# Keys and queries of a gated linear-attention kernel projected in three column blocks of 384 in place of four of 288

## The chip, the core and the metric

The kernel runs on one core of a Trainium2 chip. The core has engines with queues of their own: TensorE (PE for its matmuls, PEld for the weight loads that run beside them), VectorE (DVE), ScalarE (ACT), GpSimd (POOL) and SyncE (SP), which here only issues transfers. The metric is the device time of one execution in microseconds.

## What is computed

With x of 2048 rows and 576 columns, the reference mixes two branches by a gate for each row:

```python
def _A_ref(x, wqkv, wo):                      # linear attention, 32 heads of 18 columns
    qkv = (x @ wqkv).reshape(B, S, 3, H, Dh).transpose(2, 0, 3, 1, 4)
    q, k, v = qkv[0], qkv[1], qkv[2]
    phi = lambda t: jnp.where(t > 0, t + 1, jnp.exp(t)) + 1e-6
    pq, pk = phi(q), phi(k)
    kv = jnp.einsum("bhsd,bhse->bhde", pk, v)
    z = jnp.einsum("bhsd->bhd", pk)
    num = jnp.einsum("bhqd,bhde->bhqe", pq, kv)
    den = jnp.einsum("bhqd,bhd->bhq", pq, z)[..., None] + 1e-6
    return (num / den).transpose(0, 2, 1, 3).reshape(B, S, D) @ wo

def _B_ref(x, w1, b1, w2, b2):                # MLP, 576 -> 4608 -> 576
    h = _gelu(jnp.einsum("bsd,df->bsf", _layernorm(x), w1) + b1)
    return jnp.einsum("bsf,fd->bsd", h, w2) + b2

g = _sigmoid((x * gate_w).sum(-1, keepdims=True))
return g * _A_ref(x, wqkv, wo) + (1 - g) * _B_ref(x, w1, b1, w2, b2)
```

## The kernel before

The rows of x are cut into 16 tiles of 128. Every matmul works on numbers split into a high and a low part, so that one product is a sum of several. The 576 rows of the contraction are four slices of 128 and one of 64; with the parts this gives 14 matmuls for one block of output columns. `HI_FIRST = HH + LH + TAIL + HL` and `BY_ROWS` are two orders of the same 14: HH and TAIL need the high parts of weights and x, LH the low part of x, HL the low part of the weights, and the second matmul of TAIL a low part of the last weight slice.

**The first stage** goes over the tiles once. For each tile it projects keys and queries, applies phi, and adds to the sums that linear attention needs. Keys (576 columns) and queries (576) are each projected in two halves of 288 columns (`HALF`), so that a tile takes four blocks of 14 matmuls, 56 in all. The second half of the keys is two columns wider: the gate's weights and a column of ones stand there, and `sums_of_x` reads the gate's sum and the row's mean out of them. `phi` reads a block from its bank of ps: two ACT activations (relu of the negative, then exp) into e, and one DVE operation that puts max(p, 0) + e into k or into the tile's acc. `keys_split` and `split_xn` make high and low parts (ks, xs), and `add_products` adds the tile's 19 products into six banks of ps, in two parts of 8 and 11 matmuls. Blocks of projections alternate between banks 6 and 7 (`halves_in`). In the loop over tiles FIRST to 15, the order on PE is: keys of tile n, first part of the products of tile n-1, queries of tile n, second part of these products. Work for the MLP's input (`Y_JOBS`) is hung in by hand at 48 numbered places, three to a tile. The queries of the last `LATE` = 3 tiles are left for later: one after the loop, one after the sums have been copied out, one behind the transposes of the first normalized tile.

**The start** is written out by hand for the first three tiles. SP issues the loads of x (`load_x`, into t, one transfer for four slices and two for the last) and of the weights (`load_w`, into s); the first block of key weights is issued by ACT itself, in pieces, ahead of its table load and its first copies. `split_w` and `split_x` make the high part by ACT and the low part by DVE. Before that, PE multiplies a tile of ones 12 times (`WARM`). First all keys of the first block go to PE, then those of the second.

The framework counts transfers on eight counters, DMAHW0 to DMAHW7. A transfer that takes a counter in use waits on the issuing engine until the one before it on that counter has landed; whatever stands behind it on that engine waits too.

**Later stages**: the sums are finished and projected by wo, each tile's queries are normalized, transposed and multiplied (`attend`), and then the MLP runs for some 830 us, its instructions put in order by a planner that works on fixed costs in the code. The change does not touch that planner.

Of the kernel before, what the change touches and what calls it, by code (L numbers as in the profile page):

```python
# [9 lines left out]
F32 = mybir.dt.float32  # L10
F32R = mybir.dt.float32r
AF = mybir.ActivationFunctionType
OP = mybir.AluOpType
# [4 lines left out]
P = 128  # L18
S, D, H, DH, F = 2048, 576, 32, 18, 4608
NT = S // P  # L20
HALF = D // 2
# [14 lines left out]
EPS_LN = 1e-5  # L36
WARM = 12
FIRST = 3
LATE = 3
X_RING = 4  # L40
LAST_SHARE = 7

# [5 lines left out]
HI_FIRST = HH + LH + TAIL + HL  # L48
BY_ROWS = [p for pair in zip(HH, HL) for p in pair] + TAIL + LH
# [56 lines left out]
def half_cols(half):  # L106
    return slice(half * HALF, (half + 1) * HALF)
# [19 lines left out]
def tile_gated_mix(ctx: ExitStack, tc: tile.TileContext, x, xm, xe, wm, we, wvm, wve, wo, um, ue, w2, b1, b2, gw, out):  # L127
    nc = tc.nc
    pe, act, dve, pool = (InOrder(tc, e) for e in (nc.tensor, nc.scalar, nc.vector, nc.gpsimd))
    sp = InOrder(tc, nc.sync)  # L130
# [5 lines left out]
    ps = ctx.enter_context(tc.tile_pool(name="ps", bufs=1, space=PSUM)).tile([P, 8, 512], F32, name="ps")  # L136
# [60 lines left out]
    QUERY, KEY = range(2)  # L197
    W, at_ = {}, 0
    for part in (KEY, QUERY):
        for half in range(2):  # L200
            n = HALF + 2 * (part == KEY and half)
            W[part, half] = ym[:, at_:at_ + 10 * n].rearrange("p (a n) -> p a n", n=n)
            at_ += 10 * n
# [12 lines left out]
    yt = a1b.enter_context(tc.tile_pool(name="yt", bufs=3))  # L216
    xnp = a1b.enter_context(tc.tile_pool(name="xnp", bufs=2))
    kp = a1b.enter_context(tc.tile_pool(name="kp", bufs=2))
    wsp = wsc.enter_context(tc.tile_pool(name="wsp", bufs=4, side="right"))
    wraw, xs, xraw, xnraw = {}, {}, {}, {}  # L220

    def load_w(part, half, pieces=((0, 5),), by=sp):
        if (part, half) not in wraw:
            wraw[part, half] = wsp.tile([P, 5, HALF + 2], F32, name="s", tag="s")
        s = wraw[part, half]
        main = wm[part * 2 + half].rearrange("p (t n) -> p t n", t=4)
        tail = we[part * 2 + half]
# [6 lines left out]
    def split_w(part, half, by=dve, pieces=((0, 5),)):  # L234
        w = W[part, half]
        s = wraw[part, half][:, :, :w.shape[2]]
# [28 lines left out]

    halves_in, banks = cycle((6, 7)), {}

    def project(i, part, half, order=BY_ROWS, n=None, between={}):
        w = W[part, half]
        p = banks[i, part, half] = ps[:, next(halves_in) if n is None else n]  # L270
# [5 lines left out]
    def projected(i, part):  # L276
        for half in range(2):
            project(i, part, half)
# [12 lines left out]
    def keys_phi(i, half):  # L291
        if half == 0:
            K[i] = kp.tile([P, D], F32, name="k")
        phi(K[i], i, KEY, half, (lambda: None, lambda: sums_of_x(i))[half])

    def sums_of_x(i):
        own = slice(PLACE[i], PLACE[i] + 1)
        act.activation(gsum[:, own], banks[i, KEY, 1][:, HALF:HALF + 1], AF.Copy)
        act.activation(nmean[:, own], banks[i, KEY, 1][:, HALF + 1:HALF + 2], AF.Copy, scale=-1 / D)

    def sum_keys(i):
        if i != ORDER[0]:
# [16 lines left out]
            dve.tensor_sub(to[:, at_:at_ + c1 - c0], xnraw[i][:, c0:c1], raw(to[:, c0:c1]))  # L319

    def queries_out(i):
        for half in range(2):
            phi(acc[i], i, QUERY, half)


    KC = 448
# [136 lines left out]
    load_xn(first[0])  # L463
    load_w(QUERY, 1)
    load_xn(first[1])
    pool.memset(mask, 1.0)
    blocks = heads(mask)
# [5 lines left out]
    split_w(KEY, 0, pieces=((0, 1), (1, 2)))  # L473
    split_x(first[0], ((4, 5),))
    split_w(KEY, 0, pieces=((2, 4), (4, 5)))

    def first_keys(n, half, between={}):
        project(first[n], KEY, half, HI_FIRST, 3 * half + n, between)

    def first_queries(n, half):  # L480
        project(first[n], QUERY, half, HI_FIRST)

    def both_phi(n):
        for half in range(2):
            keys_phi(first[n], half)


    column = ps[:, 7, :5]
# [13 lines left out]
    dve.tensor_copy(wraw[KEY, 1][:, :, HALF:HALF + 1], column[:, :, None])  # L502
    dve.memset(wraw[KEY, 1][:, :, HALF + 1:HALF + 2], 1.0)
    split_w(KEY, 1)
    split_x(first[2])
    load_x(ORDER[3])
    first_keys(0, 1)
    first_keys(1, 1)
    both_phi(0)
    split_w(QUERY, 0)  # L510
    first_keys(2, 0)
    first_keys(2, 1)
    both_phi(1)
    keys_split(first[0])
    first_queries(0, 0)
    first_queries(1, 0)
    both_phi(2)
    phi(acc[first[0]], first[0], QUERY, 0)
    split_xn(first[0])
    moments_of(first[0])  # L520
    load_xn(first[2])
    first_queries(2, 0)
    phi(acc[first[1]], first[1], QUERY, 0)
    for part in range(2):
        add_products(first[0], part)
    split_w(QUERY, 1)
    phi(acc[first[2]], first[2], QUERY, 0)
    first_queries(0, 1)
    first_queries(1, 1)
    keys_split(first[1])  # L530
    split_xn(first[1])
    moments_of(first[1])
    load_xn(ORDER[FIRST])
    phi(acc[first[0]], first[0], QUERY, 1)
    add_products(first[1], 0)
    phi(acc[first[1]], first[1], QUERY, 1)
    first_queries(2, 1)
    split_x(ORDER[3])
    load_x(ORDER[4])
    load_x(ORDER[5])  # L540
    add_products(first[1], 1)
    phi(acc[first[2]], first[2], QUERY, 1)
    keys_split(first[2])
    split_xn(first[2])
    wsc.close()
# [51 lines left out]
    for n in range(FIRST, NT):  # L597
        i, before = ORDER[n], ORDER[n - 1]
        if n + 3 < NT:
            load_x(ORDER[n + 3])  # L600
        project(i, KEY, 0)
        keys_phi(i, 0)
        project(i, KEY, 1)
        if n + 1 < NT:
            split_x(ORDER[n + 1])
        keys_phi(i, 1)
        moments_of(before)
        if n + 1 < NT:
            load_xn(ORDER[n + 1])
        keys_split(i)  # L610
        add_products(before, 0)
        split_xn(i)
        run(3 * n)
        if n < NT - LATE:
            projected(i, QUERY)
# [7 lines left out]
    projected(late[0], QUERY)  # L623
    queries_out(late[0])
    moments_of(end)
    for part in range(2):
# [125 lines left out]
    normalize(2, (0,))  # L752
    transpose_q(0)
    normalize(2, (1,))
    for half in range(2):
# [861 lines left out]
```

## Time and profile before

| | |
|---|---|
| timed runs | 1095.13, 1095.46 and 1095.92 us, median 1095.46 |
| profiled execution | span 1094.1 us from its first to its last instruction; its own time around the span is not listed apart |
| PE | busy 1087.8 us of the span, 6694 matmuls |
| DVE, ACT, POOL | 917.2, 687.5, 235.6 us |
| mean granted clock | 0.999 |
| projections of keys and queries | 896 matmuls: 672 of 288 columns and 224 of 290 |

The page gives busy time by engine, the chain of work that ended last, and groups of instructions. The timeline lists instructions in order of time, those of one kind merged: start, length, engine (with q: its queue, which issues transfers), operation, tile written and tile read, shape, how many, and in brackets the idle time before and what ended it. Nearly all instructions have the line of one helper, L120, so the tiles tell them apart. A matmul's length overlaps the next one's; the pace is read from start to start.

### The profile page before, as it was taken

The numbers are of one execution on the slowest core, as the hardware profiler recorded it, in microseconds if no ns is written. First come the engines' busy times: TensorE is split into PE (matmuls) and PEld (weight loads), VectorE is DVE, ScalarE is ACT, GpSimd is POOL, SyncE is SP. The second block draws the span as 40 slices with busy tenths as digits, with TensorE's granted clock in tenths as the row PEclk, the third lists the DMA queues.
The fourth block names the chain that finished last, engine by engine and source line by source line (L and its number), as shares of the span: only waits on it lengthen the run. The fifth ranks groups of instructions, "written<-read, shape, count | busy, mean of one in ns | idle before, by whom it ended". The sixth has DMA issues, their size and how long they took to land.

```text
span 1094.1 us, 18599 instructions
## 1 busy us (share of the span) xinstructions
PE 1087.8 (99%) x6694; PEld 996.8 (91%) x6694; DVE 917.2 (84%) x1553; ACT 687.5 (63%) x1230; POOL 235.6 (22%) x232
## 2 busy tenths in 40 slices
PE   9999999999999999999999999999999999999998
PEld 9999999999898889988889999989899999999898
DVE  4568784895799999899999997988887888878888
ACT  6677765454667887777877876455545555455552
POOL 2111112531123232332111202121122211221110
PEclk9999999999999999999999999999999999999999
DMA  6466772745745565764556559574444435444432
GB/s 186 128 88 190 171 218 102 286 173 188 252 152 195 184 206 192 235 215 161 199 174 222 195 192 395 174 253 119 138 145 118 130 119 150 132 119 119 135 100 87
DMA packets 109006, 189.72 MB, mean 173 GB/s; under 512 B 8940, under 2 KB 68604, under 8 KB 104818
## 3 DMA queue, kind: packets, MB, share of 16 engines
q1 hardware_dynamic: 108002, 187.78, 53.3%
q8 instruction: 53, 0.87, 0.3%
q10 hardware_dynamic: 720, 0.74, 0.2%
q14 instruction: 39, 0.32, 0.1%
q0 software_dynamic: 192, 0.01, 0.1%
HBM read 121.70 MB, written 66.80 MB: 172 GB/s over the span
## 4 chain that ended last, share of the span: by engine, by line
PE 93%; DVE 3%; DMA 1%; ACT 1%; issue 0%; SPq 0%; ACTq 0%; DVEq 0%
PE ps L120 93%; DVE accs L120 1%; DMA s<-in_wm 0%; DVE h L120 0%; DMA fresh<-in_ue 0%; DMA ystage<-late_acc 0%; ACT u L120 0%; DMA s<-in_we 0%; DVE wp L120 0%; DVE region L120 0%; SPq L120 0%; DVE den L120 0%; DVE fresh L120 0%; DVE ystage L120 0%; DVE u L120 0%
## 5 line engine op out<-in xcount | busy, mean ns | idle before, releaser
L120 PEld LDWEIGHTS ps<-region,h 128*128 128x128 f32 x3072 | 437.8, 188 | 30.1 <-ACT ps L120 4.3
L120 PE MATMUL ps<-region,h 128*128 128x288 f32 x3072 | 457.1, 296 | 1.0 <-DVE region L120 0.4
L120 DVE TENSOR_TENSOR accs<-ps,accs 128x576 f32<-128x576 f32 x330 | 246.1, 753 | 60.9 <-PE ps L120 54.1
L120 PE MATMUL ps<-y,wa 128*128 128x512 f32 x1008 | 257.6, 393 | 0.0
L120 PEld LDWEIGHTS ps<-y,wa 128*128 128x128 f32 x1008 | 180.9, 188 | 30.3 <-ACT ps L120 0.2
L120 POOL TENSOR_TENSOR fresh<-fresh 128x288 f32<-128x288 f32 (+1 forms) x128 | 116.4, 913 | 410.5 <-DMA fresh<-in_w 129.6
L120 PE MATMUL ps<-y,wb 128*128 128x512 f32 x756 | 199.3, 394 | 0.1
L120 DVE TENSOR_TENSOR h<-u,h 128x512 fp32r<-128x512 f32 x240 | 165.9, 704 | 8.7 <-ACT u L120 8.7
L120 PEld LDWEIGHTS ps<-y,wb 128*128 128x128 f32 x756 | 133.9, 188 | 20.9 <-ACT u L120 0.5
L120 ACT ACTIVATE region<-fresh 128x576 fp32r<-128x576 f32 (+1 forms) x132 | 81.3, 625 | 73.5 <-PE ps L120 72.9
L120 PE MATMUL ps<-y 128*128 128x288 f32 (+1 forms) x896 | 125.8, 297 | 0.3 <-DVE y L120 0.2
L120 PEld LDWEIGHTS ps<-y 128*128 128x128 f32 x896 | 122.6, 189 | 1.8 <-DVE y L120 0.4
L120 ACT ACTIVATE ps<-ps 128x576 f32<-128x576 f32 (+1 forms) x127 | 78.7, 621 | 45.0 <-PE ps L120 21.5
L120 POOL TENSOR_TENSOR u<-u 128x512 f32<-128x512 f32 x44 | 57.0, 1296 | 193.5 <-DVE h L120 54.9
L120 DVE TENSOR_TENSOR region<-fresh,region 128x576 fp32r<-128x576 f32 (+1 forms) x132 | 93.8, 723 | 1.1 <-ACT region L120 1.1
L120 ACT ACTIVATE u<-ps 128x512 f32<-128x512 f32 x73 | 43.0, 589 | 68.4 <-PE ps L120 68.2
L120 ACT ACTIVATE h<-u 128x512 fp32r<-128x512 f32 x128 | 73.5, 622 | 10.0 <-DVE u L120 5.5
L120 ACT ACTIVATE h<-u,b1s 128x512 fp32r<-128x512 f32 x73 | 52.6, 722 | 42.6 <-DVE u L120 42.4
L120 PE MATMUL ps<-wp,qt 128*128 128x288 f32 x448 | 63.0, 297 | 0.0
L120 DVE TENSOR_TENSOR u<-ps,u 128x512 f32<-128x512 f32 x74 | 50.4, 683 | 13.5 <-PE ps L120 12.7
L120 PEld LDWEIGHTS ps<-wp,qt 128*128 128x128 f32 x448 | 59.8, 188 | 0.0
L120 DVE TENSOR_TENSOR u<-u 128x512 f32<-128x512 f32 x84 | 58.1, 691 | 1.7 <-POOL u L120 1.1
(137 smaller groups left out, 1052.1 us busy)
## 6 DMA issues: line engine op xcount, KB each, us to landing
w1d<-wa SPq DMA_DIRECT2D x17, 1280.0 KB
wa<-w1d SPq DMA_DIRECT2D x68, 320.0 KB
fresh<-in_w SPq DMA_DIRECT2D x70, 288.0 KB
y<-yd SPq DMA_DIRECT2D x14, 1280.0 KB
w1d<-wb SPq DMA_DIRECT2D x17, 960.0 KB
wb<-w1d SPq DMA_DIRECT2D x51, 320.0 KB
yd<-ystage SPq DMA_DIRECT2D x28, 320.0 KB
fresh<-in_um SPq DMA_DIRECT2D x64, 128.0 KB
```

Source lines behind the costliest of these rows:

```text
L120: self.last = self.tc.keep_in_program_order(op(*args, **kwargs))
```

## The change

Keys and queries of a tile are taken as one row of 1152 columns and cut into three blocks of 384 (`BLOCK`): block 0 is keys 0 to 383, block 1 the other 192 keys and the first 192 queries (`REST` = 192) with the two extra columns (386 wide), block 2 the other 384 queries. The first 192 query columns of each tile, late tiles too, are so projected with its keys. The weights still lie in memory as four pieces of 288 columns (Q0, Q1, K0, K1), so each block is loaded from two of them. `LATE` becomes 4: the fourth late block goes with the last one into banks 4 and 5. At the start, all blocks 2 of the first three tiles are projected one after another, and the products of the first and second tile follow without a projection between.

```diff
-LATE = 3
+LATE = 4
+BLOCK = 384
+REST = D - BLOCK
...
-    wsp = wsc.enter_context(tc.tile_pool(name="wsp", bufs=4, side="right"))
+    wsp = wsc.enter_context(tc.tile_pool(name="wsp", bufs=3, side="right"))
...
+    Q0, Q1, K0, K1 = range(4)
+    EDGE = BLOCK - HALF
+    SOURCES = (((K0, 0, HALF), (K1, 0, EDGE)), ((K1, EDGE, HALF), (Q0, 0, REST)), ((Q0, REST, HALF), (Q1, 0, HALF)))
+
+    def load_w(n, pieces=((0, 5),), by=sp):
+        if n not in wraw:
+            wraw[n] = wsp.tile([P, 5, BLOCK + 2], F32, name="s", tag="s")
         for t0, t1 in pieces:
-            if t0 < 4:
-                by.dma_start(s[:, t0:min(t1, 4), :HALF], main[:, t0:min(t1, 4)])
-            if t1 == 5:
-                load_twice(s[:, 4, :HALF], tail, by)
+            to = 0
+            for i, c0, c1 in SOURCES[n]:
+                s = wraw[n][:, :, to:to + c1 - c0]
+                to += c1 - c0
+                if t0 < 4:
+                    by.dma_start(s[:, t0:min(t1, 4)], wm[i].rearrange("p (t n) -> p t n", t=4)[:, t0:min(t1, 4), c0:c1])
+                if t1 == 5:
+                    load_twice(s[:, 4], we[i][:, c0:c1], by)
...
-    def phi(dst, i, part, half, also=lambda: None):
+    def phi(i, n, outs, also=lambda: None):
-        p, own = banks[i, part, half][:, :HALF], half_cols(half)
-        e = tmp.tile([P, HALF], F32, name="e")
-        act.activation(e, p, AF.Relu, scale=-1.0)
+        p = banks[i, n]
+        e = tmp.tile([P, BLOCK], F32, name="e")
+        act.activation(e, p[:, :BLOCK], AF.Relu, scale=-1.0)
         act.activation(e, e, AF.Exp, scale=-1.0)
         also()
-        dve.scalar_tensor_tensor(dst[:, own], p, 0.0, e, op0=OP.max, op1=OP.add)
+        c0 = 0
+        for dst in outs:
+            c1 = c0 + dst.shape[1]
+            dve.scalar_tensor_tensor(dst, p[:, c0:c1], 0.0, e[:, c0:c1], op0=OP.max, op1=OP.add)
+            c0 = c1
...
-    def keys_phi(i, half):
-        if half == 0:
+    def keys_phi(i, n):
+        if n == 0:
             K[i] = kp.tile([P, D], F32, name="k")
-        phi(K[i], i, KEY, half, (lambda: None, lambda: sums_of_x(i))[half])
+            phi(i, 0, [K[i][:, :BLOCK]])
+        else:
+            phi(i, 1, [K[i][:, BLOCK:], acc[i][:, :REST]], lambda: sums_of_x(i))
...
     def queries_out(i):
-        for half in range(2):
-            phi(acc[i], i, QUERY, half)
+        phi(i, 2, [acc[i][:, REST:]])
...
-    load_w(KEY, 0, ((0, 1), (1, 2), (2, 4)), act)
+    load_w(0, ((0, 1), (1, 2), (2, 4)), act)
...
-    load_w(KEY, 0, ((4, 5),), act)
+    load_w(0, ((4, 5),), act)
     load_x(first[1])
-    load_w(KEY, 1)
+    load_w(1)
     load_x(first[2])
-    load_w(QUERY, 0)
+    load_w(2)
...
-    project(late[1], QUERY, 0, n=4)
-    project(late[1], QUERY, 1, n=0)
+    project(late[1], 2, at_=4)
...
-    for half in range(2):
-        project(late[2], QUERY, half, n=4 + half)
+    for n in range(2):
+        project(late[2 + n], 2, at_=4 + n)
     transpose_q(1)
     tail_q(2)
     queries_out(late[2])
+    queries_out(late[3])
```

The first place is ACT's queue at the very start. Rows name the tile written and the tensor read, the shape of one instruction, and in brackets what it waits for; in_wm and in_we hold the four main slices and the last slice of the weights. Before, ACT has three pieces and the last slice, twice, to issue:

```order
L120 DMA s<-in_wm 128x288 x2
L120 DMA s<-in_wm 128x2x288
L120 ACT_TABLE_LOAD
L120 ACTIVATE tiny<-ones 128x1 [waits DVE_49]
L120 DMA s<-in_we 64x288 [waits DMAHW1_49]
L120 DMA s<-in_we 64x288 [waits DMAHW3_49]
L120 ACTIVATE y<-t 128x512
```

After the change, on the same engine, from its third instruction on (the first two are the pieces of 288 and 96 columns of the slice before):

```order
L122 DMA s<-in_wm 128x288
L122 DMA s<-in_wm 128x96
L122 DMA s<-in_wm 128x2x288 [waits DMAHW0_49]
L122 DMA s<-in_wm 128x2x96 [waits DMAHW2_49]
L122 ACT_TABLE_LOAD
L122 ACTIVATE tiny<-ones 128x1 [waits DVE_49]
L122 DMA s<-in_we 64x288 [waits DMAHW6_49]
L122 DMA s<-in_we 64x288 [waits DMAHW0_49]
L122 DMA s<-in_we 64x96 [waits DMAHW2_49]
L122 DMA s<-in_we 64x96 [waits DMAHW3_49]
L122 ACTIVATE y<-t 128x512 [waits DMAHW1_49]
```

ACT issues ten transfers where it issued five, and six of them wait for a counter where two did, all ahead of its table load or of its first copy.

The second place is SP's queue behind the loads of x for the first two tiles, up to the load of x for the third; here the second block of weights is issued. Before:

```order
L120 DMA t<-in_xe 64x128 [waits DMAHW0_49]
L120 DMA s<-in_wm 128x4x288 [waits DMAHW2_49]
L120 DMA s<-in_we 64x288 [waits DMAHW4_49]
L120 DMA s<-in_we 64x288 [waits DMAHW5_49]
L120 DMA t<-in_xm 128x512 [waits DMAHW6_49]
```

After:

```order
L122 DMA t<-in_xe 64x128 [waits DMAHW3_49]
L122 DMA s<-in_wm 128x4x192 [waits DMAHW4_49]
L122 DMA s<-in_we 64x192 [waits DMAHW5_49]
L122 DMA s<-in_we 64x192 [waits DMAHW7_49]
L122 DMA s<-in_wm 128x4x192 [waits DMAHW1_49]
L122 DMA s<-in_we 64x192 [waits DMAHW4_49]
L122 DMA s<-in_we 64x192 [waits DMAHW5_49]
L122 DMA t<-in_xm 128x512 [waits DMAHW6_49]
```

Three transfers became six, and the load of x for the third tile stands behind all of them.

More of the change, by code (lines that the diff above doesn't have):

```diff
@@ L196, in tile_gated_mix @@
     Y = ym.rearrange("p (m j s n) -> p m j s n", m=7, j=TPB, s=5)
-    QUERY, KEY = range(2)
-    W, at_ = {}, 0
-    for part in (KEY, QUERY):
-        for half in range(2):
-            n = HALF + 2 * (part == KEY and half)
-            W[part, half] = ym[:, at_:at_ + 10 * n].rearrange("p (a n) -> p a n", n=n)
-            at_ += 10 * n
+    W, at_ = [], 0
+    for n in (BLOCK, BLOCK + 2, BLOCK):
+        W.append(ym[:, at_:at_ + 10 * n].rearrange("p (a n) -> p a n", n=n))
+        at_ += 10 * n
     y_place = ym[:, at_ + X_RING * 9 * P:][:, :2 * 5 * P]
@@ L218, in tile_gated_mix, with split_w @@
     kp = a1b.enter_context(tc.tile_pool(name="kp", bufs=2))
-    wsp = wsc.enter_context(tc.tile_pool(name="wsp", bufs=4, side="right"))
+    wsp = wsc.enter_context(tc.tile_pool(name="wsp", bufs=3, side="right"))
     wraw, xs, xraw, xnraw = {}, {}, {}, {}
[L222 to L227, printed above, removed]
-        for t0, t1 in pieces:
-            if t0 < 4:
-                by.dma_start(s[:, t0:min(t1, 4), :HALF], main[:, t0:min(t1, 4)])
-            if t1 == 5:
-                load_twice(s[:, 4, :HALF], tail, by)
-    def split_w(part, half, by=dve, pieces=((0, 5),)):
-        w = W[part, half]
-        s = wraw[part, half][:, :, :w.shape[2]]
+    Q0, Q1, K0, K1 = range(4)
[4 more added lines that the diff above has]
+            wraw[n] = wsp.tile([P, 5, BLOCK + 2], F32, name="s", tag="s")
+        for t0, t1 in pieces:
+            to = 0
[6 more added lines that the diff above has]
+                    load_twice(s[:, 4], we[i][:, c0:c1], by)
+    def split_w(n, by=dve, pieces=((0, 5),)):
+        w = W[n]
+        s = wraw[n][:, :, :w.shape[2]]
         for t0, t1 in pieces:
@@ L266, in tile_gated_mix, with project @@
     halves_in, banks = cycle((6, 7)), {}
-    def project(i, part, half, order=BY_ROWS, n=None, between={}):
-        w = W[part, half]
-        p = banks[i, part, half] = ps[:, next(halves_in) if n is None else n]
+    def project(i, n, order=BY_ROWS, at_=None, between={}):
+        w = W[n]
+        p = banks[i, n] = ps[:, next(halves_in) if at_ is None else at_]
         for m, (a, b) in enumerate(order):
@@ L472, in tile_gated_mix, with first_keys, first_queries @@
     split_x(first[0], ((0, 4),))
-    split_w(KEY, 0, pieces=((0, 1), (1, 2)))
+    split_w(0, pieces=((0, 1), (1, 2)))
     split_x(first[0], ((4, 5),))
[L475 to L481, printed above, removed]
+    split_w(0, pieces=((2, 4), (4, 5)))
+    def first_keys(n, block, between={}):
+        project(first[n], block, HI_FIRST, 3 * block + n, between)
+    def first_queries(n):
+        project(first[n], 2, HI_FIRST)
     def both_phi(n):
-        for half in range(2):
-            keys_phi(first[n], half)
+        for block in range(2):
+            keys_phi(first[n], block)
     column = ps[:, 7, :5]
@@ L501, in tile_gated_mix @@
     first_keys(1, 0)
[L502 to L504 removed]
+    dve.tensor_copy(wraw[1][:, :, BLOCK:BLOCK + 1], column[:, :, None])
+    dve.memset(wraw[1][:, :, BLOCK + 1:BLOCK + 2], 1.0)
+    split_w(1)
     split_x(first[2])
@@ L514, in tile_gated_mix @@
     keys_split(first[0])
-    first_queries(0, 0)
-    first_queries(1, 0)
+    first_queries(0)
+    first_queries(1)
     both_phi(2)
-    phi(acc[first[0]], first[0], QUERY, 0)
+    queries_out(first[0])
     split_xn(first[0])
@@ L521, in tile_gated_mix @@
     load_xn(first[2])
-    first_queries(2, 0)
-    phi(acc[first[1]], first[1], QUERY, 0)
+    first_queries(2)
+    queries_out(first[1])
     for part in range(2):
         add_products(first[0], part)
[L526 to L529, printed above, removed]
     keys_split(first[1])
@@ L533, in tile_gated_mix @@
     load_xn(ORDER[FIRST])
-    phi(acc[first[0]], first[0], QUERY, 1)
+    queries_out(first[2])
     add_products(first[1], 0)
-    phi(acc[first[1]], first[1], QUERY, 1)
-    first_queries(2, 1)
     split_x(ORDER[3])
@@ L622, in tile_gated_mix @@
     late, end = ORDER[NT - LATE:], ORDER[-1]
-    projected(late[0], QUERY)
+    project(late[0], 2)
     queries_out(late[0])
```

18 lines of the change are left out of this document (6 added, 12 removed).

## The prediction

> **What bounds the kernel now.** I read the page first, then the stages by windows, then PE's waits, then the chain of waits, and last the timeline of the first 14 us and of one tile of the loop.
>
> ```profile
> PE 1087.8 (99%) x6694; PEld 996.8 (91%) x6694; DVE 917.2 (84%) x1553; ACT 687.5 (63%) x1230; POOL 235.6 (22%) x232
> ```
>
> ```profile
> 55.00:166.00 111.00, 111.00 (x739) 106.47 (x738) 84.95 (x182) 80.18 (x180) 18.08 (x14) 1.00 0.68 166
> 166.00:201.00 35.00, 34.84 (x220) 31.23 (x219) 18.61 (x44) 14.61 (x33) 8.01 (x6) 1.00 0.37 130
> 201.00:1094.00 893.00, 888.28 (x5390) 807.71 (x5388) 785.48 (x1263) 555.59 (x937) 199.25 (x192) 1.00 0.53 177
> ```
>
> The columns are stretch, length, then PE, PEld, DVE, ACT and POOL. In the loop over tiles PE is busy for all of 111.00 us, while DVE stands at 84.95 and ACT at 80.18. In the stretch behind it PE loses 0.16 us. So in the stage that the change touches PE is the bound: what makes its work shorter is gained, what makes it start later is lost, and work taken from ACT and DVE is worth nothing.
>
> ```profile
> 1.74 5.12 DMA s<-in_wm
> 6.88 0.48 SPq L120
> 7.40 2.97 DMA s<-in_we
> 10.47 1.43 ACT y L120
> 11.93 1.68 DVE y L120
> 13.65 179.71 PE ps L120 x1201
> ```
>
> The chain (start, length, what) shows where a late start would come in: transfers of weights, ACT's copy and DVE's rest of them, and from 13.65 us on PE alone for 180 us. Nothing gives back a delay before 13.65.
>
> **The change part by part: the matmuls.** The columns that PE must stream stay the same, since 4 x 288 = 3 x 384. What falls away is a fixed share of each matmul: 42 for 56 in each of 16 tiles.
>
> ```profile
> 59.70 1.58 PE L120 MATMUL ps<-ks,xs 128*128 128x448 f32 x7
> 61.12 3.90 PE L120 MATMUL ps<-y 128*128 128x288 f32 x28
> 64.86 0.85 PE L120 MATMUL ps<-xs,ks 128*128 128x512 f32 x3
> 65.54 1.23 PE L120 MATMUL ps<-ks,xs 128*128 128x512 f32 x5
> 66.61 3.88 PE L120 MATMUL ps<-y 128*128 128x288 f32 x28
> 70.33 2.16 PE L120 MATMUL ps<-ks,xs 128*128 128x64 f32 x11
> ```
>
> From start to start, 28 matmuls of 288 columns take 70.33 - 66.61 = 3.72 us, 132.9 ns each; 7 of 448 take 61.12 - 59.70 = 1.42, 202.9 each; 3 of 512 take 65.54 - 64.86 = 0.68, 226.7 each. There is no gap between blocks, so nothing else is saved there. 384 lies between 288 and 448, and the line through these gives 132.9 + 96 x 0.4375 = 174.9 ns. The line to 512 gives 173.1, and pure proportion 177.2. A tile takes 56 x 132.9 = 7442 ns now. With 174.9 it takes 42 x 174.9 = 7346, 96 ns less, and 16 tiles give 1.5 us. The ends are 0 (177.2) and 2.8 us (173.1). I take 1.5, by the two nearest rows.
>
> The Trainium skill, "TensorE: Matmul & The Clock Gate", section "Wait — 56ns, not 53.3ns?", gives N / 2.4 GHz plus about 2.5 ns a matmul. By it 14 fewer would bring 35 ns a tile, 0.6 us in all; it would also have 288 columns at 122.5 ns, where the rows show 132.9, so the rows are used.
>
> **The start.** Here the change adds work ahead of PE.
>
> ```profile
> 0.81 1.38 ACTq L120 DMA_DIRECT2D s<-in_wm  x3
> 2.23 1.28 ACT L120 ACT_TABLE_LOAD   x1 [2.23 <-issue]
> 3.52 0.20 ACT L120 ACTIVATE tiny<-ones 128x1 f32<-128x1 f32 x1
> 4.24 1.17 ACTq L120 DMA_DIRECT2D s<-in_we  x2
> 5.46 0.63 ACT L120 ACTIVATE y<-t 128x512 fp32r<-128x512 f32 x1 [1.74 <-DMA t<-in_xe]
> ...
> 6.88 0.69 ACT L120 ACTIVATE y<-s 128x576 fp32r<-128x576 f32 x1
> 7.99 0.45 ACT L120 ACTIVATE y<-s 128x288 fp32r<-128x288 f32 x1 [0.43 <-DMA s<-in_we]
> ```
>
> ```profile
> 4.45 0.47 SPq L120 DMA_DIRECT2D t<-in_xe  x1
> 4.96 0.72 SPq L120 DMA_DIRECT2D s<-in_wm  x1
> ```
>
> ACT had finished tiny at 3.72 and issued the next transfer only at 4.24: it waited for its counter (DMAHW1). SP's two rows are its first that wait for DMAHW0 and DMAHW2, so both were free by 4.45 and 4.96. The first wait now stands with ACT's fifth transfer, ahead of everything else that ACT does. Step by step: four issues of 0.46 (1.38 / 3) from 0.81 end at 2.65; the fifth waits for DMAHW0 to 4.45 and ends at 4.91; the sixth waits for DMAHW2 and ends at 5.42; table load and tiny (1.28 + 0.20) end at 6.90. Then come four issues for the last slice at 0.585 (1.17 / 2). Without any wait they end at 9.24. The second to fourth reuse the counters of the fifth and sixth and of the second tile's x, all issued between 4.45 and 5. A landing after issue took 2.97 in the chain, and for ACT's second issue of the last slice (4.24 + 0.585 = 4.83) 7.99 - 4.83 = 3.2; the 288 KB piece issued at 1.74 among the first crowd took 5.12. With 3.2 the second issue starts at 7.65, and the four end at 9.4; with 5.12 at 11.3. I take 9.4, since by 4.45 fewer transfers stand ahead. So ACT's first copy moves from 5.46 to 9.4 (9.2 to 11.3).
>
> ```profile
> 7.73 1.20 DVE L120 TENSOR_TENSOR y<-s,y 128x576 fp32r<-128x576 f32 x2
> ```
>
> ```profile
> L120 ACT ACTIVATE y<-s x7: 427/685/1419, 6.0 to 26.1; 128x288 fp32r<-128x288 f32 x3, 128x1440 fp32r<-128x1440 f32 x2, 128x576 fp32r<-128x576 f32 x1, 128x1450 fp32r<-128x1450 f32 x1
> L120 DVE TENSOR_TENSOR y<-s,y x7: 451/753/1669, 6.7 to 27.5; 128x288 fp32r<-128x288 f32 x3, 128x1440 fp32r<-128x1440 f32 x2, 128x576 fp32r<-128x576 f32 x1, 128x1450 fp32r<-128x1450 f32 x1
> ```
>
> (The last two are the tile s: shortest, middle and longest in ns.) DVE had the low parts of the first block done at 8.93, 3.47 us behind ACT's first copy. The 480 columns that the four pieces gain cost DVE (1669 - 451) / (1450 - 288) = 1.05 ns each, 0.5 us, so PE has all of the first block at 9.4 + 3.97 = 13.4. Of tile one's first 14 matmuls the last five need that; then come 14 of the next tile, and 19 x 0.175 end at 16.7. By then 28 x 384 = 10,752 columns are through.
>
> ```profile
> 1.13 5.49 PE L120 MATMUL ps<-ones 128*128 128x128 f32 x24 [1.13 <-DVE ones L120]
> 6.48 0.61 PE L120 MATMUL ps<-y 128*128 128x288 f32 x1
> 6.88 0.52 PE L120 MATMUL ps<-ones 128*128 128x128 f32 x2
> ...
> 7.37 0.38 PE L120 MATMUL ps<-ones 128*128 128x128 f32 x2
> ...
> 8.70 4.74 PE L120 MATMUL ps<-y 128*128 128x288 f32 x33
> 13.65 0.40 PE L120 MATMUL ps<-y 128*128 128x290 f32 x1 [0.21 <-DVE y L120]
> ```
>
> Before, 4 + 33 matmuls of 288, or 10,656 columns, were through when PE went on at 13.65. The loss is 16.7 - 13.65 = 3.1 us, and 2.9 to 5.0 with the ends of ACT's first copy. The second block does not add to it: SP's six issues put its last landing at about 13.2 by the same landing times, ACT copies 1930 columns in 1.8 us (1419 ns for 1450, and 0.85 ns more for each column) and DVE takes 2.2, which ends near 17.3; PE asks for it at its tenth matmul of that block, 16.7 + 9 x 0.175 = 18.3.
>
> **PE's pace after a pause.** The first 24 passes over ones take 5.49 / 24 = 0.23 us each; the pair at 6.88 takes 0.52 us, the same pair at 7.37 only 0.38. So PE ran at about half its pace for its first 6 us and then at the full one. After the change it has nothing to do from 6.6 (1.13 + 5.49) to about 10.0, where before it had work at once. Whether the slow pace holds or returns then is not shown. At half pace until 16.1 (six us from 10.0, as at first) the first 14 matmuls end at 16.3 and the next 14 at 18.7: 2.0 us more. The lower end is 0, and later stalls at the slow pace could bring it to 2.3. I take 1.4, because the first six us began cold and these may begin half warm.
>
> The Trainium skill, "TensorE: Matmul & The Clock Gate", "Part 1: The HAM clock gate", says that PE's clock falls to half after an idle window of some 3.4 us and comes back after a busy one; the trace agrees in the factor of two, while its windows put the granted clock at 1.00 throughout, so this slow pace is not seen in that column.
>
> **The rest** is hidden. phi's 3 x 2 activations for 4 x 2 lie on ACT, and the split output on DVE (block 1 writes twice), which have 31 and 26 us to spare in the 111. A bank was asked for again after 14 matmuls and eight products, 1.86 + 1.75 (66.61 - 64.86) = 3.6 us; now it is after 2.45 + 1.75 = 4.2 at the earliest. Tile 12 loses its queries behind the keys, but each late tile keeps a third of them, so PE's time for a late tile grows by 28 x 174.9 ns - 3.72 us = 1.2 us, which gives DVE room.
>
> ```profile
> 30.11 0.82 DVE L120 TENSOR_TENSOR xs<-xn,xs 128x512 fp32r<-128x512 f32 x2
> 33.11 0.86 PE L120 MATMUL ps<-xs,ks 128*128 128x512 f32 x3
> ...
> 181.38 1.47 ACT L120 ACTIVATE accs<-ps 128x448 f32<-128x448 f32 x3
> ...
> 181.95 3.96 PE L120 MATMUL ps<-y 128*128 128x288 f32 x28
> ```
>
> At the start, the second tile's products now follow the first's at once. Before, DVE had its xs at 30.93 and PE asked at 33.11, 2.2 us of room. The 28 query matmuls between (3.7 us) go, the 42 ahead grow by 42 x 42 ns = 1.8, and ACT no longer copies a weight block there (1.4); the room left is about 1.7 us, an estimate. Behind the stage, the copies of the sums end at 182.85, 0.9 us into the late queries that run from 181.95; these now last 14 x 174.9 ns = 2.4 us instead of 3.7 and still cover them. If this cover is gone, it costs what is missing, under 1 us.
>
> **Sum**: +3.1 (start) + 1.4 (pace) - 1.5 (fixed shares) = +3.0 us on the profiled span of 1094.1. The timed median lies 1.4 above that span for what surrounds it; I move it equally, to 1098.5. A change under 0.2% (2.2 us) can hardly be told from none here.
>
> **The rivals.**
> - PE's pace holds through the pause. It is the same late start without the 1.4: +1.6, 1097.1. For it speaks that PE was nearly warm when the pause begins; against it, that the pace needed six us of work at first.
> - The start is not late, because transfers land sooner or ACT posts its issues without waiting. Then only the fixed shares count: 1095.5 - 1.5 = 1094.0, or 1092.7 with their upper end. Against it: ACT's own issues and table load, without any wait, take 6 x 0.46 + 1.48 + 4 x 0.585 = 6.6 us from 0.81. It decides itself by ACT's first copy; before 6.0 us this rival holds.
> - A new wait inside the stage: the products of tile two, or of the last tile, ask for ks or xs before DVE has them. With the 1.7 us of room gone and 1.5 more lost it gives 1098.5 + 1.5 = 1100.0. Nothing in the loop of before shows such a wait; the two places are new orders.
>
> **How the numbers follow.** Late start with some slow pace 0.53, pace held 0.27, start not late 0.10, new wait 0.10. The first has its own range of 1097.5 to 1100.3, and lies over +0.2% for nearly all of it; pace held is mostly within 0.2%; the start not late is half within, half faster. Faster: 0.05. Same: 0.05 + 0.21 + 0.03 = 0.29, slower the rest, 0.66. The range for 8 in 10 leaves out the start not late and the longest delays: 1096.0 to 1100.5.
>
> **What would show it.** Right: ACT's first copy y<-t at 9.2 to 11.3 us; the first 28 projections through at 16.7 to 19; 28 matmuls of 384 from start to start in 4.85 to 4.95 us; a loop tile 0.1 us shorter than 11.2; PE without waits from 19 to 190. Wrong: a first copy before 6 us, 384 columns at 177 ns or under 170, or PE's waits for ks and xs.

## The result, and the profile after

The changed kernel takes 1102.88 us (median of four runs, 1102.46 to 1103.39), the kernel before 1095.69 beside it (four runs, 1095.13 to 1097.07): 1.0061 of its time, interval 1.0049 to 1.0073. It is slower, as forecast, but by 7 us where 3 were predicted and outside the range that was given.

The page and the windows of the changed kernel, in the columns of before:

```profile
PE 1090.6 (99%) x6470; PEld 998.8 (91%) x6470; DVE 917.7 (83%) x1552; ACT 682.0 (62%) x1197; POOL 234.8 (21%) x232
```

```profile
55.00:166.00 111.00, 111.00 (x607) 106.06 (x606) 82.44 (x189) 77.98 (x161) 17.46 (x14) 1.00 0.68 172
166.00:201.00 35.00, 35.00 (x207) 32.51 (x206) 18.74 (x45) 16.97 (x37) 7.02 (x5) 1.00 0.37 129
201.00:1094.00 893.00, 891.97 (x5391) 809.73 (x5390) 788.40 (x1268) 557.93 (x941) 201.34 (x193) 1.00 0.54 177
```

PE has 224 matmuls fewer and is busy for longer. In the loop it is as full as before, and DVE and ACT have 2.5 and 2.2 us less to do there, which is worth nothing. So the loss does not lie in the loop. The chain of waits (start, length, what) puts it at the start:

```profile
0.81 3.56 DMA s<-in_wm
4.40 4.08 DMA s<-in_wm
9.01 0.61 ACTq L122
9.66 0.61 ACTq L122
10.32 1.05 ACT y L122 x2
11.41 188.17 PE ps L122 x1025
```

PE alone now carries the chain from 11.41 us on. Ahead of it stand two landings of weights and ACT's last two issues. Here is ACT's timeline:

```profile
0.81 4.62 ACTq L122 DMA_DIRECT2D s<-in_wm  x6
5.46 1.28 ACT L122 ACT_TABLE_LOAD   x1 [5.46 <-DMA s<-in_wm]
6.32 0.53 ACTq L122 DMA_DIRECT2D s<-in_we  x1
6.75 0.20 ACT L122 ACTIVATE tiny<-ones 128x1 f32<-128x1 f32 x1
8.50 1.77 ACTq L122 DMA_DIRECT2D s<-in_we  x3
10.32 0.63 ACT L122 ACTIVATE y<-t 128x512 fp32r<-128x512 f32 x1 [3.36 <-issue]
```

The six issues take 4.62 us because the fifth waits for a landing. The last slice's second issue could start only at 8.50. It takes the counter of the fifth transfer (the row with DMAHW0 in the queue's order), which went out at 4.40 and landed 4.08 us later, at 8.48. So ACT's first copy comes at 10.32 in place of 5.46, and PE waits:

```profile
PE ps L122 <- ACT y L122: 4.8, 1, 4.8
...
PE ps L122 <- DVE region L122: 0.4, 1, 0.4
PE ps L122 <- ACT ps L122: 0.3, 1, 0.3
```

The rows name who ended the wait, then the us in all, the times and the longest. The first row is the start, the other two belong to the MLP. PE waits for neither ks nor xs anywhere. What the pause of 4.8 us does to PE is in narrow windows over the start. After the stretch come its length and PE's busy time with its instructions; the third number from the right is the granted clock:

```profile
9.00:10.00 1.00, 0.00 (x0) 0.00 (x0) 0.00 (x0) 0.00 (x0) 0.00 (x0) 1.00 1.04 279
10.00:11.00 1.00, 0.00 (x0) 0.00 (x0) 0.02 (x1) 0.68 (x2) 0.00 (x0) 0.57 1.06 254
11.00:12.00 1.00, 0.59 (x2) 0.59 (x3) 1.00 (x2) 1.00 (x4) 0.00 (x0) 0.50 0.84 211
18.00:20.00 2.00, 2.00 (x8) 2.00 (x7) 2.00 (x2) 1.25 (x3) 0.00 (x0) 0.50 1.08 334
20.00:21.00 1.00, 1.00 (x7) 1.00 (x6) 1.00 (x3) 0.00 (x0) 0.00 (x0) 0.81 0.87 270
21.00:22.00 1.00, 1.00 (x7) 1.00 (x6) 0.14 (x1) 0.00 (x0) 0.00 (x0) 1.00 1.02 372
```

The clock falls to 0.50 within the tenth microsecond (0.57 for that whole stretch puts it at 10.14) and is back within the twentieth (0.81 puts it at 20.38). The trace's own record of it says full pace from 6.72, half from 10.13 and full again from 20.37. That is 10.24 us at half pace, nine of them with work: some 8 matmuls of 384 columns in 2 us there, 320 ns from start to start, against 176 behind it.

Two rows of the timeline show the new matmul in the loop:

```profile
68.83 5.09 PE L122 MATMUL ps<-y 128*128 128x384 f32 x28
73.75 0.86 PE L122 MATMUL ps<-xs,ks 128*128 128x512 f32 x3
```

28 of them take 73.75 - 68.83 = 4.92 us, 175.7 ns each.

A mark for what the start costs is the first product of the query stage (`ps<-wp,qt`), the same instruction in all kernels: it starts at 205.49 us before and at 212.92 after, 7.4 later. The first 28 x 384 columns are through at 21.68 after, 8.0 us behind the like number before (13.65). So the rest of the stage gave back about 0.6, and the later stages 0.3 (spans 1101.2 and 1094.1).

### The profile page after: what moved, and what is told of

Read it like the earlier page. It is cut to its first block, busy times and chain, and to the rows that moved or that the text cites. A ratio compares the mean times of both kernels' runs of the same rounds, so it can differ in the third digit from the quotient of the medians.

```text
span 1101.2 us, 18134 instructions
## 1 busy us (share of the span) xinstructions
PE 1090.6 (99%) x6470; PEld 998.8 (91%) x6470; DVE 917.7 (83%) x1552; ACT 682.0 (62%) x1197; POOL 234.8 (21%) x232
## 4 chain that ended last, share of the span: by engine, by line
PE 94%; DVE 2%; DMA 1%; ACT 1%; issue 0%; SPq 0%; ACTq 0%; DVEq 0%
PE ps L122 94%; DMA s<-in_wm 1%; DVE accs L122 1%; DVE h L122 0%; DMA fresh<-in_ue 0%; ACT u L122 0%; DVE wp L122 0%; DVE region L122 0%; DVE den L122 0%; DVE fresh L122 0%; DVE u L122 0%; SPq L122 0%; DVE wa L122 0%; ACT h L122 0%; ACTq L122 0%
## 5 line engine op out<-in xcount | busy, mean ns | idle before, releaser
L122 PE MATMUL ps<-y 128*128 128x384 f32 (+1 forms) x672 | 127.2, 345 | 4.9 <-ACT y L122 4.8
```

Of the source, the lines that this page charges most:

```text
L122: self.last = self.tc.keep_in_program_order(op(*args, **kwargs))
```

## The experiments

The table has all kernels: time, the median of the kernel before beside it, ratio, and from each one's trace the start of ACT's first copy, of the first projection, the stretch at half pace that follows the warm-up, and the start of that first product of the query stage. The last four columns belong to one execution of each kernel.

| kernel | us | before | ratio (95%) | copy | projection | half pace | mark |
|---|---|---|---|---|---|---|---|
| before | 1095.46 | | | 5.46 | 6.47 | none | 205.49 |
| after | 1102.88 | 1095.69 | 1.0061 (1.0049–1.0073) | 10.32 | 11.41 | 10.13–20.37 | 212.92 |
| e1_warm | 1099.75 | 1095.80 | 1.0038 (1.0024–1.0052) | 10.01 | 11.11 | none | 209.41 |
| e2_whole | 1097.77 | 1095.80 | 1.0018 (1.0009–1.0027) | 6.42 | 7.51 | none | 207.64 |
| e3_late3 | 1097.83 | 1095.80 | 1.0020 (1.0011–1.0029) | 6.18 | 7.28 | 7.50–14.32 | 207.82 |
| e4_split | 1100.56 | 1095.80 | 1.0045 (1.0032–1.0057) | 8.31 | 9.32 | 10.39–17.22 | 211.19 |
| e5_early | 1097.17 | 1096.21 | 1.0009 (1.0000–1.0018) | 4.38 | 6.11 | none | 206.79 |
| e6_early_warm | 1096.89 | 1096.21 | 1.0004 (0.9995–1.0013) | 4.30 | 7.37 | none | 206.26 |
| e7_before_early | 1096.27 | 1096.21 | 1.0002 (0.9993–1.0011) | 4.06 | 6.27 | none | 206.41 |
| e8_before_warm2 | 1097.42 | 1096.21 | 1.0013 (1.0005–1.0022) | 5.45 | 6.47 | from the start to 13.80 | 207.76 |
| e9_pool | 1099.91 | 1096.02 | 1.0039 (1.0027–1.0052) | 6.76 | 7.84 | 9.28–16.11 | 209.56 |
| e10_pool_warm | 1098.63 | 1096.02 | 1.0020 (1.0011–1.0029) | 6.66 | 7.74 | 12.16–15.57 | 208.71 |
| e11_whole_pool | 1096.92 | 1096.02 | 1.0010 (1.0002–1.0019) | 4.29 | 6.18 | none | 205.93 |

My theory after the result: the start is late, by the number of transfers that ACT issues and their waits for counters, and PE's pause then costs a long stretch at half pace. The rival: it is the bytes, since a first block of 384 columns needs a third more before PE can go on; then neither the count of transfers nor the pace matters much. A third part of the change, the fourth late tile, could cost too.

**e1_warm: the changed kernel without the pause.**

```diff
-WARM = 12
+WARM = 34
```

> The changed kernel with 34 products of ones ahead of the first projection in place of 12, so that PE has no pause between 6.6 and 11.4 us; nothing else. Theory (late start plus half pace after the pause): ACT's first copy stays near 10.3 us, PE keeps full pace, the first 28 projections end near 18.0 us instead of 21.7, and the time falls by 3.7 us to about 1099.2. Rival (the pace is not set by the pause, the whole delay lies in the transfers): no change, 1102.9.

The warm-up now lasts until the first projection. The pause shrinks from 4.80 to 0.37 us (PE's timeline):

```profile
11.11 0.44 PE L122 MATMUL ps<-y 128*128 128x384 f32 x1 [0.37 <-ACT y L122]
...
12.45 0.44 PE L122 MATMUL ps<-y 128*128 128x384 f32 x1 [0.27 <-ACT y L122]
...
13.62 8.63 PE L122 MATMUL ps<-y 128*128 128x384 f32 x46
```

ACT's copies stand almost where they were (the first 0.3 us earlier), no stretch is at half pace, and 3.1 us of the 7.2 are gone by the medians (2.5 by the ratios) where 3.7 were expected; the mark moves by 3.5, of which the earlier copy can be 0.3. This is the price of the pace, measured with the late start left in, and above the 1.4 that I had forecast by any of the three. What remains is the start itself at full pace: the first 28 matmuls of 384 columns are through at 17.96 us, where the next one starts, 4.3 behind before.

**e2_whole: as few transfers as before.** The weights are laid out in memory as three pieces of 384 columns, so that a block is loaded from one piece; the bytes that PE must wait for stay those of the changed kernel.

```diff
-    Q0, Q1, K0, K1 = range(4)
-    EDGE = BLOCK - HALF
-    SOURCES = (((K0, 0, HALF), (K1, 0, EDGE)), ((K1, EDGE, HALF), (Q0, 0, REST)), ((Q0, REST, HALF), (Q1, 0, HALF)))
+    SOURCES = tuple(((n, 0, BLOCK),) for n in range(3))
...
-    wm, we = cut(np.asarray(A_wqkv)[:, :2 * D], 4)
+    wm, we = cut(np.concatenate([np.asarray(A_wqkv)[:, D:2 * D], np.asarray(A_wqkv)[:, :D]], axis=1), 3)
```

> The changed kernel with the weights laid out in memory as its own three blocks of 384 columns, so that every block is loaded with as many transfers as before the change, each a third larger; nothing else. Theory (the number of transfers on ACT's queue and their waits for counters): ACT's first copy back at 5.5 to 6 us, no pause, 1095.5 + 0.5 (wider first block) - 0.6 (fewer matmuls) = 1095.4, 1094.6 to 1096.2. Rival 1 (a first block of 960 KB in place of 720 KB is what comes late): 1099 or more. Rival 2 (block order, late queries): 1102.

5.1 of the 7.2 us go with the number of transfers, and in the execution traced the half pace too. But 2.0 stay where none were expected: the time lies between the theory's range and the rival's. The first copy is still 1 us late, and ACT's second half of the last slice lands late (chain, and PE's timeline):

```profile
5.77 5.66 DMA s<-in_we
```

```profile
12.10 0.44 PE L122 MATMUL ps<-y 128*128 128x384 f32 x1 [1.10 <-ACT y L122]
12.69 9.54 PE L122 MATMUL ps<-y 128*128 128x384 f32 x51 [0.15 <-DVE y L122]
```

Issued at 5.77, it went out behind the main slices of the second block, and took 5.66 us to land, where the last slice's in the kernel before took 3.2. That fits a part for the rival, the bytes; no run separates them from the order in which the transfers went out.

**e3_late3: three late tiles again.** On top of e2, `LATE` goes back from 4 to 3.

```diff
-LATE = 4
+LATE = 3
...
-    for n in range(2):
+    for n in range(1):
         project(late[2 + n], 2, at_=4 + n)
...
-    queries_out(late[3])
```

> As the kernel with the weights laid out in three blocks, and three late tiles in place of four; nothing else. Theory (late tiles do not matter): within 0.4 us of the four late tiles. Rival (the fourth late block fills a wait behind the stage, or adds one): 0.5 us or more to either side.

1097.83 against 1097.77: the fourth late tile costs and brings nothing that can be seen. The profiled execution had a half-paced stretch that e2's had not; of this kernel's eleven runs four show a mean clock of 0.997 or 0.998, and of e2's eleven also four.

**e4_split: more transfers, on the kernel before.** Each transfer of weights is cut into one of 192 and one of 96 columns; all blocks stay 288 wide.

```diff
-            if t0 < 4:
-                by.dma_start(s[:, t0:min(t1, 4), :HALF], main[:, t0:min(t1, 4)])
-            if t1 == 5:
-                load_twice(s[:, 4, :HALF], tail, by)
+            for c0, c1 in ((0, 192), (192, HALF)):
+                if t0 < 4:
+                    by.dma_start(s[:, t0:min(t1, 4), c0:c1], main[:, t0:min(t1, 4), c0:c1])
+                if t1 == 5:
+                    load_twice(s[:, 4, c0:c1], tail[:, c0:c1], by)
```

> The kernel before, with four blocks of 288 columns, where each transfer of these weights is cut into two, of 192 and 96 columns; nothing else. Theory (the number of transfers ahead of ACT's first copy): first copy at 9.5 to 10.5 us, half pace for some 10 us, time 1095.5 + 4.4 (late copy) + 3.0 (pace) - 0.4 (a short wait that falls away) = 1102.5. Rival (blocks of 384 and their order cause the delay): 1095.5 to 1096.5.

Same bytes, same matmuls, and 4.8 us slower. So cutting the transfers does most of the damage without any wider block, and again through both parts, a first copy at 8.31 and a half-paced stretch; copy, stretch and time all stay under what was expected. The pieces are shorter as well as more here; e9 below takes issues from ACT and leaves the pieces as they are. The gap that PE has here (2.70 us) is shorter than in the changed kernel (4.80), and so is the stretch (6.83 us for 10.24):

```profile
9.32 0.40 PE L120 MATMUL ps<-y 128*128 128x288 f32 x1 [2.70 <-ACT y L120]
```

**e8_before_warm2: a pause and hardly any warm-up, on the kernel before.**

```diff
-WARM = 12
+WARM = 2
```

> Edit: the kernel before with 2 warm-up products, so that TensorE pauses from about 2 us to about 6.5 us and nothing else changes. Theory (a pause of over about 4 us ahead of the projections is followed by a stretch at half pace): granted clock 0.5 over 3.4 to 10.2 us behind 6.5 us, time 1097.0 to 1100.5 us. Rival (the pause alone costs nothing; in the changed kernel the wider products or the late data gave the half pace): 1095.3 to 1096.3 us, clock 1.00 after 7 us.

ACT's first copy and the first projection stand where they stood, to 0.01 us. PE's timeline and its windows:

```profile
6.47 0.61 PE L120 MATMUL ps<-y 128*128 128x288 f32 x1 [4.12 <-ACT y L120]
```

```profile
12.00:13.00 1.00, 1.00 (x6) 1.00 (x6) 0.98 (x1) 0.97 (x3) 0.00 (x0) 1.00 1.05 317
14.00:15.00 1.00, 1.00 (x10) 1.00 (x9) 0.92 (x3) 0.00 (x0) 0.00 (x0) 1.00 1.04 309
```

Six matmuls of 288 columns in the one microsecond, ten in the other: PE runs at half pace until 13.80, where the trace's first record of the clock stands, and yet the column says 1.00. So the expectation held in time (1097.0 to 1100.5) and pace, and failed in what the column would show. It does not show what it was made for, though: that first record is a rise, and no fall stands ahead of it. PE never came to full pace before the pause, so the run prices a missing warm-up and not a pause that takes the pace away. For that stand the changed kernel, whose record has full pace from 6.72 and half from 10.13, and e1, which fills the pause and keeps the pace. The kernel is 1.2 us slower, interval 0.5 to 2.4, with nothing late; its mark moves by 2.3. The kernel before was itself slow up to its first record at 7.14, so 6.7 us at half pace are added, where the changed kernel works at half pace for 9.0.

**e5_early and e6_early_warm: e2 with its late slice mended.** SP issues the last slice right behind x of the first tile; e6 adds four warm-up products (`WARM = 16`).

```diff
     act.activation(tiny, ones[:, 0:1], AF.Exp)
-    load_w(0, ((4, 5),), act)
+    load_w(0, ((4, 5),))
```

> Edit: e2_whole with the last slice of the first weight block (its fifth slice, in pieces) issued by SP right behind x of the first tile, instead of by ACT ahead of its table load; ACT then has three issues before the table load. Theory (what e2 still loses is the wait of the late tail, 1.25 us of idle PE, and ACT's issue waiting for a landing): first copy at 4.7 to 5.5 us, no wait of 1 us on ACT's second tail copy, 1095.0 to 1096.3 us. Rival (the bytes of a 384-column first block and of the tile's x decide, whoever issues them): another transfer is late in its place, time stays at 1097.2 to 1098.0 us.

> Edit: e5_early with 16 warm-up products in place of the former number, so that no pause of TensorE is left ahead of the first projection. Theory: in e5 no stretch at half pace is left, so nothing is gained: within 0.5 us of e5. Rival (e5 still has a half-paced stretch in some executions): 1 to 3 us faster than e5.

ACT's first copy now stands at 4.38, earlier than before the change. By the ratios e5 gains 1 us on e2, and its PE is still idle in places. PE's timeline, and then ACT's:

```profile
8.39 0.44 PE L122 MATMUL ps<-y 128*128 128x384 f32 x1 [1.25 <-ACT y L122]
...
14.80 1.88 PE L122 MATMUL ps<-y 128*128 128x386 f32 x9 [0.76 <-ACT y L122]
17.01 5.25 PE L122 MATMUL ps<-y 128*128 128x386 f32 x28 [0.33 <-DVE y L122]
```

```profile
7.30 0.31 ACT L122 ACTIVATE y<-t 128x128 fp32r<-128x128 f32 x1 [1.47 <-DMA t<-in_xe]
...
12.94 1.81 ACT L122 ACTIVATE y<-s 128x1930 fp32r<-128x1930 f32 x1 [3.46 <-DMA s<-in_we]
```

The last weight slice keeps nobody waiting any more. In its place x's last slice is late, and then the second block, whose copy starts at 12.94 where it started at 10.47 before the change. Here the rival of e5 is right as to the mechanism; its time began 0.03 us above what was measured. e6 is 0.3 us faster than e5, less than the runs can separate. It is the only wide kernel whose interval reaches below 1; e5's begins at 1.0000.

**e7_before_early: the same edit on the kernel before.**

> Edit: the kernel before, with the last slice of the first key block issued by SP right behind x of the first tile. Control for e5. Theory: in the kernel before the tail is no late transfer, so 1095.0 to 1096.0 us, no change. Rival (ACT's issues set the first copy there too): first copy up to 0.8 us earlier and 1094.3 to 1095.0 us.

The first copy moves up by 1.40 us and the time not at all. But the second block's copy now comes at 11.40 for 10.47, and PE stops for it:

```profile
12.87 1.49 PE L120 MATMUL ps<-y 128*128 128x290 f32 x9 [1.03 <-ACT y L120]
```

So an earlier first copy alone gained nothing before the change; whether it would with the second block in time is not shown.

**e9_pool and e10_pool_warm: the changed kernel, mended in its own layout.** POOL issues the last slice's four transfers; e10 also has 20 warm-up products.

```diff
+    load_w(0, ((4, 5),), pool)
     pool.dma_start(gwr[:, :D], gw.rearrange("(a n) -> a n", a=1))
...
     act.activation(tiny, ones[:, 0:1], AF.Exp)
-    load_w(0, ((4, 5),), act)
```

> Edit: the changed kernel with the four transfers of the first block's last slice issued by POOL, ahead of its two for the gate, instead of by ACT behind its table load. ACT keeps six issues, POOL has six. Theory (the late first copy is ACT's queue: its tail issues wait for earlier landings): first copy at 6 to 8 us in place of 10.3, the pause of PE under 3 us, the half-paced stretch shorter or gone, 1097.5 to 1099.5 us. Rival (the bytes and the pieces themselves land late, whoever issues them): first copy 8 to 9.5 us, time 1100 to 1102 us.

> Edit: e9_pool with 20 warm-up products for 12. Theory (the half pace comes from the pause alone): no half-paced stretch behind the warm-up, 1096.8 to 1098.2 us, up to 2 us below e9. Rival (e9 has no pause left to be filled): equal to e9 within 0.5 us, or up to 1 us above, by the longer warm-up.

With the four issues out of ACT's queue its first copy comes at 6.76, as the theory had it. The time stands 3.3 us closer to the kernel before than the changed kernel's, between the theory's range (to 1099.5) and the rival's (from 1100). PE still stops (the first two rows are e9's, the last e10's):

```profile
7.84 0.44 PE L122 MATMUL ps<-y 128*128 128x384 f32 x1 [1.52 <-ACT y L122]
...
10.33 0.69 PE L122 MATMUL ps<-y 128*128 128x384 f32 x1 [1.38 <-ACT y L122]
```

```profile
10.45 0.44 PE L122 MATMUL ps<-y 128*128 128x384 f32 x1 [1.23 <-ACT y L122]
```

The stop at 10.3 is the third and fourth slice, issued fifth and sixth on ACT, from 4.29 us on, behind a landing. Since the pieces of e9 are those of the changed kernel, the 3.3 us are what it costs to have the last slice's issues stand in ACT's queue, pause and pace with them. e10 missed its range by 0.4 us. Its eleven runs suggest why: four have a mean clock of 1.000 and take 1096.37 to 1097.37 us, six have 0.998 (1098.42 to 1099.06), one 0.996 (1099.38). The traced one, at 0.998, has one stretch of 3.41 us at half pace. If the clock tells the others apart as well, such a stretch costs this kernel about 1.4 us, and it falls into it in some executions and not in others.

**e11_whole_pool: both mends and few transfers.** e2 with the slice on POOL and 14 warm-up products.

> Edit: e2_whole (weights laid out as three blocks of 384, so that a block is four transfers again) with the first block's last slice issued by POOL, and 14 warm-up products. Theory (with neither late issues nor a pause left, the bytes of a 384-column first block, 246 KB more, still cost about 0.8 us at some 320 GB/s, and 0.6 us come back in the key stage): 1095.6 to 1096.8 us, same as before. Rival (wider blocks gain once the start is mended): under 1095.3 us.

```profile
8.23 0.45 PE L122 MATMUL ps<-y 128*128 128x384 f32 x1 [1.01 <-ACT y L122]
...
16.19 6.09 PE L122 MATMUL ps<-y 128*128 128x386 f32 x33 [0.35 <-DVE y L122]
```

1096.92 us is 0.9 above the kernel before (interval 0.2 to 2.1), 0.1 outside the theory's range, and not under 1095.3. Two of its runs (0.998 and 0.997 in clock) took 1098.62 and 1100.27; the other nine lie between 1095.98 and 1097.19. The first copy stands 1.2 us earlier than before the change, but the copy of x's last slice comes at 7.13 for 6.66, and the second block's at 12.11 for 10.47. No version with 384 columns beat the kernel before. That the bytes are what is left here was argued from these times; no run had a narrow first block and wide later ones.

## Why the prediction was wrong in size

The direction, the place and the mechanism were as forecast; three terms of the sum were mis-sized, all to the same side. The largest error is in the pace, the second in the start.

- **Start, +3.1 taken, 2.9 to 5.0 allowed.** It measures 4.3 to 4.5: 4.3 by e1's matmuls, and 4.5 by e1's mark (209.41 - 205.49 = 3.9, plus the 0.6 of the fixed shares). The first copy came at 10.32, inside 9.2 to 11.3 but 0.9 above the 9.4 that I chose. The step that failed is the landing time of the fifth transfer: I gave it the 3.2 us that a piece of 72 KB had taken before, and it carries 288 KB and took 4.08. Whether its size or the other transfers on the way made the difference, no run separates. The step behind the copy was short by 0.6 more. With e1's copy at 10.01 it puts the first block whole at 13.98 and, with 19 matmuls left, ends at 17.3; it took until 17.96, because by then five matmuls were through (the sixth starts at 13.90) and not nine. PE had waited for ACT once more at 12.45, 0.27 us, and had its passes over ones and the gate's transposes in between.
- **Pace, +1.4 taken, 0 to 2.3 allowed.** It measures 2.5 to 3.1 by e1's time, and 3.2 to 3.5 by its mark. This is the largest miss, and the upper end was wrong too. I let the half pace end at 16.1, six us after PE's restart as in its cold start; it ended at 20.37, 9 us after the restart. The cold start was the wrong model: PE was at full pace from 6.72 and lost it in the pause, and the pace came back only after a whole step of 3.41 us full of projections. And I read the granted clock of 1.00 during the cold warm-up as a sign that the column does not show the pace. It shows it from the first record on; ahead of that it prints 1.00 at any pace, as e8 repeats. The Trainium skill, "TensorE: Matmul & The Clock Gate", "Part 1: The HAM clock gate", says that the clock falls to half after an idle stretch of 3.4 us and comes back after a busy one of that length, counted in windows that run on by themselves. The trace agrees with the fall (10.13, 3.5 us after the warm-up's end at 6.62), though e3 and e10 lost their clock to shorter stops (below). From 10.13 the steps of 3.41 us end at 13.54, 16.96 and 20.37: the first begins with 1.28 us of the pause, and the second is all work but did not bring the clock back, so that "after a busy one" would have given 16.96 and not 20.37.
- **Fixed shares, -1.5 taken, 0 to -2.8 allowed.** About -0.6: 28 matmuls take 4.92 us, as forecast (4.85 to 4.95), but 175.7 ns each and not 174.9, and 42 x 175.7 = 7.38 us a tile are 62 ns under the 7.44 of before. Over 16 tiles that would be 1.0 us; the stage gave back 8.0 - 7.4 = 0.6 us in all, and where the other 0.4 went is not shown. Interpolating between 288 and 448 columns was good to half a per cent, and that half per cent was a third of the gain (34 of 96 ns a tile). The Trainium skill, "TensorE: Matmul & The Clock Gate", in "Wait — 56ns, not 53.3ns?", has a fixed cost of 2.5 ns a matmul. The estimate by it, 0.6 us, agrees with the total, but its 35 ns a tile do not agree with the 62 of the rows, nor its 162.5 ns for 384 columns with 175.7.
- **The rest, at nothing.** Right: PE waits nowhere for ks or xs, and e3 shows that the fourth late tile costs nothing.

The sum by what was measured is 4.5 + 3.5 - 0.6 - 0.3 = +7.1 on the span, 1094.1 to 1101.2; it closes by construction, since the marks set its terms. The rivals fell: the pace did not hold, the start was late, and no new wait came up inside the stage.

## What to carry to other kernels

A block that is built from two pieces of memory doubles the transfers of its load; where an engine both issues transfers and does the first copies, count the issue that has to wait for a counter and give it a landing time measured on a transfer of its own size, not the shortest in sight (4.08 us for 288 KB here, where 3.2 had been taken from 72 KB). A late start is paid twice if PE pauses in it: look at the granted clock in narrow windows behind every pause, and distrust the column only ahead of its first record. When a gain is the difference of two nearly equal products (56 x 132.9 and 42 x 175 ns), an interpolated price is not good enough to size it.

## What the runs showed of the hardware

By the traces' own records, the clock at the start held each state for 3.41 us or a multiple: half pace for 3.41 (e10), 6.83 (e3, e4, e9) or 10.24 us (after). Where such a step begins differs from trace to trace: the warm-up starts at 1.12 or 1.13 us in all, yet, e8 left out, the first rise to full pace stands anywhere from 4.08 (e3) to 7.14 us (before). So it is likely, though no second trace of one kernel shows it, that the same kernel falls into a slow step in some executions and not in others.

In four traces a step at half pace was full of work, held the five transposes of one column, and did not bring the full clock, though PE counts as busy: 13.54 to 16.96 in the changed kernel (the transposes run from 14.27 to 14.89), and steps of e3, e4 and e8 (7.50 to 10.91, 10.39 to 13.80, and 6.97 to 10.39, counted back from 13.80). The next one, full of projections, did. In e9 the step with the transposes held 1.05 us of a wait too. In e10 the slow step held projections alone, and the full clock came at its end.

A fall did not need a whole step without work. The first row is e2's, which kept its clock, the second e3's, which lost it, the last two e10's, which lost it at 12.16 (PE's timelines):

```profile
7.51 0.45 PE L122 MATMUL ps<-y 128*128 128x384 f32 x1 [1.66 <-ACT y L122]
```

```profile
7.28 0.52 PE L122 MATMUL ps<-y 128*128 128x384 f32 x1 [1.80 <-ACT y L122]
```

```profile
10.45 0.44 PE L122 MATMUL ps<-y 128*128 128x384 f32 x1 [1.23 <-ACT y L122]
...
11.22 0.47 PE L122 MATMUL ps<-accs 1*128 1x1 f32 x5
```

So a pause of half such a step can be enough, if it falls into one step (4.08 to 7.50 in e3, 4.89 to 8.30 in e2). The length of the pause alone does not decide: e10's stop of 1.23 us was shorter than e2's, but the five transposes stand in the same step, 8.75 to 12.16. These traces make no threshold, and no run took the transposes out.
